# V copies moved to GpSimd, an earlier first cast of the keys, global-query work two slots later, and a last tile in other banks

## The chip, the cores and the metric

One core of a Trainium2 chip runs the whole kernel. The metric is the device time of one execution in microseconds (us); less is better. Engines are named as in the profile: PE is TensorE's matmuls and PEld its weight loads, DVE is VectorE, ACT is ScalarE, POOL is GpSimd, SP is SyncE, which here only issues DMAs. POOL issues DMAs as well.

## The reference

Two layers, cut to what is computed:

```python
# attention: B=8, H=8, 512 local tokens, 32 global tokens, head size 64
k_all = concat([k_g, k_l]); v_all = concat([v_g, v_l])
out_g = softmax(scale * q_g @ k_all.T) @ v_all                # global queries see all keys
s_ll  = where(|i - j| <= 32, scale * q_l @ k_l.T, -1e9)       # local queries: a band of 32 each way
out_l = softmax(concat([scale * q_l @ k_g.T, s_ll])) @ v_all  # and the 32 global keys
x = concat([out_g, out_l]) as (4352, 512)
# mixture of 8 experts, weights P by 8 rounds of Sinkhorn on exp(x @ w_gate)
out = sum over e of P[:, e] * (relu(x @ w1[e]) @ w2[e])       # 512 -> 1024 -> 512
```

## The kernel before

Attention works in units: unit n is one pair of heads (hp = n % 4) of one batch (b = n // 4), 32 in all. A loop over slots s = 0..33 writes out the order of the work by hand, and each engine runs its own instructions strictly in that order. In slot s stand the scores of unit s, the following steps of units s-1 and s-2, and the preparation of unit s+1:

- st_A(n): PE transposes keys and queries of unit n; DVE writes the keys to a buffer kTe (L279), ACT writes the queries to qbd (L283). There are four kTe buffers, used in turn.
- st_B(n, part): scores in three parts (PE L299, L301), masked on DVE (L306, tile ms), exponentials on ACT (L309, tile Pu).
- st_D1(n): a copy of the global part (DVE L315, tile Pl), transposes of the local part (PE L318), copied by DVE (L320, tile pw).
- st_D2(n, n2): transposes of Pl for n (ACT copy pg, L334) and of the finished rows xn for n2 into xT (ACT L336).
- st_E(n): the products with V (PE L352), written here E(n). They read V in two alignments, va and vb, and the global V in vgz; DVE divides (L356, L357). The result sits in the pool ps_po, which has one buffer.
- Global queries come in 16 groups j of four heads: st_G1 (scores on PE L371 in the same pool ps_po, maximum on DVE L373, exponential on ACT L376), st_G2 (transposes L384, ACT copy pgs L386, one buffer), st_G3 (products L396, L397; DVE L399 and L406 and ACT L409 write xgn). G1 of group j stands in slot 2j+2, G2 and G3 in slot 2j+3. st_G4 transposes xgn.
- keep_busy(n): n filler matmuls (L465).
- f1 and f2, from slot 5: first and second layer of experts 0 and 1 (L435, L449) for batches whose attention is done. Their rows go to memory by SP (yd).

V of a batch is loaded into va by POOL's DMAs (load_v: first, mid), a small piece into vb (last); the rest of vb is a copy of va to other partitions (part). For batch 0 one half of this copy runs on POOL in slot 1 (L177, L178) and the other on DVE in slot 2 (L180), just ahead of E(0); for batch 1 both halves run on POOL in slot 4. From batch 2 on, SP's DMAs make the copy and load vgz (move), in the slot before the batch's first.

Before slot 0 stand the first loads, memsets on DVE (clear), band masks on POOL (L258), the casts of the first queries and keys to fp16 (L470), st_A(0), the transposes of the global keys (cast L211, then L218, L220) and st_A(1). After the attention come the Sinkhorn rounds and experts 2 to 7 in a form with fewer products (L768, L864). The very last second-layer tile is computed by plain (L835) in two halves of 256 columns that lie in two banks of one tile, each read by DVE (L838).

Of the kernel before, what the change touches and what calls it, by code (L numbers as in the profile page):

```python
# [10 lines left out]
FP16 = mybir.dt.float16  # L11
FP32 = mybir.dt.float32
# [11 lines left out]
def kernel(  # L24
# [13 lines left out]
    nc = tc.nc  # L38

    B, H, Sl, Dh = q_l.shape  # L40
# [87 lines left out]
    with ExitStack() as att:  # L128
# [8 lines left out]
        kgT = att_c.tile([P, HP, B * Sg], FP16)  # L137
        qgT = att_c.tile([P, HP, B * Sg], FP16)
        qbd = [att_c.tile([P, NHB, P], FP16, name=f"qbd{i}") for i in range(2)]
        kTe = [att_c.tile([P, W + Sl + W], FP16, name=f"kTe{i}") for i in range(4)]  # L140
        vgr = [att_c.tile([P, 4 * H * VW], FP16, name=f"vgz{i}") for i in range(2)]
        vgz = [t.rearrange("p (a h v) -> p a h v", a=4, h=H) for t in vgr]
        vab = [(att_c.tile([P, NJ, H, VW], FP16, name=f"va{i}"),
# [16 lines left out]
        def load_v(b):  # L160
            va, vb = vab[b % 2]
            vz = vgz[b % 2]
            src = v_l[b].rearrange("h s d -> s h d")

            def first():
                nc.gpsimd.dma_start(out=vg16[b], in_=v_g[b].rearrange("h g d -> g h d"))
                nc.gpsimd.dma_start(out=va[W:P, 0, :, 0:Dh], in_=src[0:96])

            def mid(j):
                nc.gpsimd.dma_start(out=va[:, j, :, 0:Dh], in_=src[P * j - W : P * j + 96])  # L170

            def last():
                nc.gpsimd.dma_start(out=vb[HB : HB + W, NJ - 1, :, 0:Dh], in_=src[Sl - W : Sl])

            def part(eng, lo):
                if lo:
                    eng.tensor_copy(out=vb[96:P, NJ - 1], in_=va[W : 2 * W, 0])  # L177
                    eng.tensor_copy(out=vb[0:HB, :], in_=va[HB:P, :])  # L178
                else:
                    eng.tensor_copy(out=vb[HB:P, 0 : NJ - 1], in_=va[0:HB, 1:NJ])  # L180

            def move():
                if b < 2:
                    return part
                nc.sync.dma_start(out=vb[96:P, NJ - 1], in_=va[W : 2 * W, 0])
                nc.sync.dma_start(out=vb[0:HB, :], in_=va[HB:P, :])
                nc.sync.dma_start(out=vb[HB:P, 0 : NJ - 1], in_=va[0:HB, 1:NJ])
                if b > 1:
                    load_vz(b)

            return [first] + [lambda j=j: mid(j) for j in range(1, NJ)] + [last, move]
# [30 lines left out]
        def run(steps):  # L222
            for f in steps:
                f()
# [7 lines left out]
                eng.dma_start(out=fh[t][:, h], in_=src[0, h].rearrange("(p s) d -> p s d", s=NJ))  # L232
        load_gf(0, "kgs", f0[:, 2, :], (nc.sync, nc.scalar, nc.sync, nc.scalar))
        load_gf(0, "qgs", f0[:, 3, :], (nc.sync,) * 4)
        run(load_qk(0, 2, 4, H))
        nc.vector.memset(ones_f, 1.0)
        nc.scalar.activation(out=ones_f[:, 0:1], in_=ones_f[:, 0:1], func=AF.Exp, scale=0.0)
        nc.vector.memset(mask, 0.0)
# [6 lines left out]
        def clear(i, eng):  # L245
            va, vb = vab[i]
            eng.memset(va[0:W, 0], 0.0)
            eng.memset(va[:, :, :, Dh:VW], 1.0)
            eng.memset(vb[:, :, :, Dh:VW], 1.0)
            eng.memset(vgr[i].bitcast(mybir.dt.uint32), 0)  # L250
            for j in range(4):
                eng.memset(vgz[i][W * j : W * (j + 1), j, :, Dh:VW], 1.0)

        clear(0, nc.vector)
        for a in range(2):
            band = mask[HB * a : HB * (a + 1), 1, 0:KW]
            for base, m, c in ((0, -1, 1), (2 * W, 1, -1)):
                nc.gpsimd.affine_select(out=band, in_=band, compare_op=ALU.is_ge, fill=NEG, base=base,  # L258
                                        pattern=[[c, KW]], channel_multiplier=m)
        *steps, move = load_v(0)  # L260
        part = move()
        steps[0]()
        load_vz(0)
        run(steps[1:])
        clear(1, nc.gpsimd)

        st = {}

        def st_A(n):
            b, hp = divmod(n, HP)  # L270
            qs, ks = staged[b]
            qb, kt = qbd[n % 2], kTe[n % 4]
            pt = [ps_tr.tile([P, Sl], FP16, tag="tr", name="pk"), ps_sc.tile([P, Sl], FP16, tag="sc", name="pq")]
            for t, src in enumerate((ks, qs)):
                for so in range(NJ):
                    for a in range(2):
                        nc.tensor.transpose(pt[t][HB * a : HB * (a + 1), P * so : P * (so + 1)],  # L277
                                            src[:, 2 * hp + a, so, :], identity)
            nc.vector.tensor_copy(out=kt[:, W : W + Sl].rearrange("c (p s) -> c p s", s=NJ),  # L279
                                  in_=pt[0].rearrange("c (s p) -> c p s", s=NJ))  # L280
            for a in range(2):
                r = slice(HB * a, HB * (a + 1))
                nc.scalar.copy(out=qb[r, :, HB * a : HB * (a + 1)].rearrange("c i (p s) -> c i p s", s=NJ),  # L283
                               in_=pt[1][r].rearrange("c (s i p) -> c i p s", s=NJ, i=NHB))

        def st_B(n, part):
            b, hp = divmod(n, HP)
            qb, kt = qbd[n % 2], kTe[n % 4]
            if part == 0:
                st[n] = dict(Pu=att_wk.tile([P, NHB, SW], FP16, tag="Pu", name="Pu"),  # L290
                             mx=att_wk.tile([P, NHB], FP32, tag="mx", name="mx"))
# [70 lines left out]
        def st_G1(b, g):  # L362
            n0 = HP * b + 2 * g
            gc = slice(Sg * b, Sg * (b + 1))
            sg = ps_po.tile([P, 2 * 512], FP32, tag="po")
            for c0, c1, k0 in ((0, Sl - W, 2 * W), (Sl - W, Sl, W), (Sl, S, None)):
                for hh in range(4):
                    pr, a = divmod(hh, 2)
                    r = slice(HB * a, HB * (a + 1))
                    rhs = kgT[r, 2 * g + pr, gc] if k0 is None else kTe[(n0 + pr) % 4][r, k0 : k0 + c1 - c0]  # L370
                    nc.tensor.matmul(sg[W * hh : W * (hh + 1), c0:c1], qgT[r, 2 * g + pr, gc], rhs, start=True, stop=True)  # L371
            m2 = att_wk.tile([P, 2], FP32, tag="m2")
            nc.vector.reduce_max(out=m2[:, 0:1], in_=sg[:, 0:S], axis=AX.X)  # L373
            nc.vector.tensor_scalar(out=m2[:, 1:2], in0=m2[:, 0:1], scalar1=-scale, scalar2=None, op0=ALU.mult)
            Pg = att_wk.tile([P, S], FP16, tag="Pg")
            nc.scalar.activation(out=Pg, in_=sg[:, 0:S], func=AF.Exp, scale=scale, bias=m2[:, 1:2])  # L376
            gs[(b, g)] = Pg
# [88 lines left out]

        queue = []
        NU = B * HP
        for t in range(2):
            (nc.vector.tensor_copy if t else nc.scalar.copy)(out=staged[0][t][:, 0:2], in_=fh[t])  # L470
        nc.vector.tensor_copy(out=mask[:, 0, 0:KW], in_=mask[:, 1, 0:KW])
        nc.vector.tensor_copy(out=mask[:, 2, 0:KW], in_=mask[:, 1, 0:KW])
        nc.vector.memset(mask[:, 0, 0:W], NEG)
        nc.vector.memset(mask[:, 2, 3 * W : KW], NEG)
        st_A(0)
        cast_g("kgs")
        transpose_g(0, "kgs")
        st_A(1)
        for s in range(NU + 2):
            b, hp = divmod(s, HP)  # L480
            if s < NU and b + 1 < B:
                if hp == 0:
                    queue = load_qk(b + 1, 0, 4, H)
                if hp == 2:
                    *loads, move = load_v(b + 1)
                    queue += loads
                if hp == 3:
                    if s == 3:
                        part = move()
                    else:  # L490
                        queue = [move] + queue
                if s == 4:
                    queue += [lambda: wts.__setitem__(1, [load_w1(1)]), lambda: part(nc.gpsimd, True),
                              lambda: part(nc.gpsimd, False), lambda: wts[0].append(load_w2(0))]
# [3 lines left out]
                    queue += [lambda: wts[1].append(load_w2(1))]  # L498
                take = 0 if s == 0 else 2 if s >= 8 and hp < 2 else len(queue)
                if s == 1:  # L500
                    queue += [lambda: part(nc.gpsimd, True), load_first]
                    take = len(queue)
                for i, f in enumerate(queue[:take]):
                    f()
# [29 lines left out]
                    p_l2(*l2[n2], eng)  # L534
                    n2 += 1

            g_odd = s % 2 == 1 and 3 <= s <= NU + 1
            if g_odd:
                gb, gg = divmod((s - 3) // 2, 2)
            even = s % 2 == 0 and 2 <= s <= NU  # L540
            f1("a")
            if s < NU:
                st_B(s, 0)
            if even:
                st_G1(*divmod((s - 2) // 2, 2))
            if 1 <= s <= NU:
                st_D1(s - 1)
            if g_odd:
                st_G2(gb, gg)
            f2("a")  # L550
            if s < 7:
                st_B(s, 1)
# [6 lines left out]
            f1("a")  # L559
            if 0 < s < 7:  # L560
                st_A(s + 1)
            if s == 2:
                part(nc.vector, False)
                st_E(0)
            if s == 3:
                st_D2(None, 1)
            if s == 0:
                cast_g("qgs")
            if s == 1:
                transpose_g(0, "qgs")  # L570
            f1("v")
            if s < NU:
# [1 line left out]
            if s + 1 < NU and s >= 7:  # L574
                st_A(s + 1)
            if s == 2:
                keep_busy(3)
            if 2 <= s <= NU:
                st_E(s - 1)
            f2("a")  # L580
            if s >= 6 and (s - 6) % 4 == 0:
                logits(NJ * ((s - 6) // 4), NJ)
            if g_odd:
                st_G3(gb, gg)
            if s == 8:
                transpose_g(1, "kgs")
                transpose_g(1, "qgs")
            if s == 18:
                st_G4(0)
            f1("v")  # L590
            if 1 <= s < 5:
# [66 lines left out]
    with tc.tile_pool(name="tpool", bufs=2) as tpool, \  # L658
# [169 lines left out]
        def plain(u, last):  # L828
            order = sorted(range(FT), key=lambda fk: (fk % HF == HF - 1, fk))
            for j in range(2):  # L830
                zz = ps_z.tile([P, 2, D], FP32, tag="z", name="zp")
                for i, (d0, d1) in enumerate(((0, H2), (H2, D)) if last and j else ((0, D),)):
                    z = zz[:, i, :]
                    for n, fk in enumerate(order):
                        nc.tensor.matmul(z[:, d0:d1], u.a[2 * j + fk // HF][:, fk % HF, :], work["last"][:, fk, d0:d1],  # L835
                                         start=(n == 0), stop=(n == FT - 1), skip_group_check=True)
# [208 lines left out]
```

## Time and profile before

| | |
|---|---|
| Median of 3 runs | 1020.97 us (1020.89 to 1021.79) |
| The profiled execution's own time | 1019.79 us |
| Its span in the profile | 1018.0 us |
| Granted TensorE clock, mean of the span | 0.998 |
| PE idle in slot 2 (18.75 to 27.96) | 2.06 us |
| Start of slot 8 | 65.59 us |
| Last group's G1, G3 | 315.21 us, 329.68 us |
| Last DVE read of the last tile | 1014.28 us, 0.48 us long |

A row of the timeline is: start in us from the start of the span, duration in us, engine, line of the kernel, operation, the tile written and those read, shape, and the number of merged instructions; in brackets the idle time of that engine before it and who ended it.

### The profile page before, as it was taken

The page shows a single profiled execution, that of the slowest core. Times are in us where ns is not written, and L with a number is a line of the kernel's source. Part 1 is how long each engine was busy: PE and PEld are TensorE (multiplying, and loading weights), DVE is VectorE, ACT ScalarE, POOL GpSimd, SP SyncE. Part 2 cuts the span into 40 slices and gives each one's busy share as a digit, 9 for nine tenths or more (in the row PEclk, how much of TensorE's full clock was granted, in tenths as well). Part 3 has the DMA queues.
Part 4 walks back from the last instruction along what each step waited for, and adds up shares of the span by engine and source line. Part 5 has one row for each costly group of instructions (what it writes and reads, how often), then busy time and mean ns, then how long its engine had stood idle before and what let it go on. Part 6 is the DMA issues. An engine that isn't in the chain of part 4 may idle for free.

```text
span 1018.0 us, 22071 instructions
## 1 busy us (share of the span) xinstructions
PE 992.3 (97%) x8673; PEld 644.0 (63%) x8673; DVE 780.4 (77%) x1892; ACT 636.0 (62%) x1348; POOL 296.1 (29%) x357
## 2 busy tenths in 40 slices
PE   5899999999999999999999999999999999999997
PEld 3556666665655545666666666676767676766764
DVE  7776666666664563789999888997889999888885
ACT  6777777777775556765555555556765555555551
POOL 9547886778870022111111111111111111100000
PEclk9999999999999999999999999999999999999999
DMA  9999999999961297564443333466665533123043
GB/s 170 176 169 176 203 214 224 200 193 213 228 167 42 125 236 189 141 154 120 114 114 73 73 73 73 115 184 159 156 145 119 117 75 87 48 68 73 1 105 125
DMA packets 135881, 138.40 MB, mean 136 GB/s; under 512 B 54432, under 2 KB 107872, under 8 KB 133728
## 3 DMA queue, kind: packets, MB, share of 16 engines
q0 software_dynamic: 105696, 87.32, 49.0%
q1 hardware_dynamic: 29248, 49.28, 15.1%
q8 instruction: 68, 1.11, 0.4%
q10 hardware_dynamic: 832, 0.39, 0.1%
q14 instruction: 37, 0.30, 0.1%
HBM read 144.20 MB, written 39.58 MB: 181 GB/s over the span
## 4 chain that ended last, share of the span: by engine, by line
PE 92%; DVE 3%; DMA 2%; POOL 1%; ACT 1%; issue 1%; DVEq 0%; POOLq 0%; ACTq 0%
PE z L768 29%; PE pa L864 17%; PE py L449 11%; PE ph L435 11%; PE pb L864 9%; PE pc L864 5%; DMA va<-in_v_l_dram 2%; PE zp L835 1%; PE po L352 1%; PE sc L299 1%; PE ptw L318 1%; PE pk L277 1%; PE tgx L328 1%; PE po L396 1%; DVE ms L306 1%
## 5 line engine op out<-in xcount | busy, mean ns | idle before, releaser
L768 PEld LDWEIGHTS <-hs 128*128 128x128 f16 x2264 | 220.7, 98 | 92.8 <-issue 1.1
L768 PE MATMUL z<-w2e,hs 128*128 128x256 f16 x1304 | 195.6, 273 | 0.9 <-DVE oy L802 0.9
L768 PE MATMUL z<-v,hs 128*128 128x256 f16 x960 | 144.0, 273 | 0.0
L435 PE MATMUL ph<-xT,w1e 128*128 128x512 f16 (+1 forms) x576 | 129.6, 367 | 2.1 <-DVE lg L424 1.4
L449 PE MATMUL py<-w2e,hT 128*128 128x512 f16 x544 | 128.2, 379 | 0.4 <-DVE hT L440 0.4
L789 ACT COPY z<-z 128x256 f32<-128x256 f32 x98 | 35.0, 357 | 141.9 <-PE z L768 141.9
L864 PEld LDWEIGHTS <-w1e 128*128 128x128 f16 x960 | 86.6, 97 | 57.8 <-issue 1.6
L864 PE MATMUL pa<-t,s 128*128 128x512 f16 x384 | 114.2, 379 | 0.2 <-ACT s L889 0.2
L684 POOL DMA_DIRECT2D w1e<-in_moe_w_dram x24 | 17.4, 733 | 306.2 <-PE pa L864 230.3
L309 ACT ACTIVATE Pu<-ms,mx 128x160 f16<-128x160 f32 x256 | 92.2, 424 | 21.7 <-DVE mx L306 19.0
L802 DVE SCALAR_TENSOR_TENSOR oy<-z,lg,oy 128x512 f32<-128x512 f32 x128 | 95.8, 748 | 7.4 <-ACT oy L807 5.2
L764 DVE TENSOR_TENSOR hs<-hs 128x512 f16<-128x512 f16 x224 | 94.9, 424 | 8.2
L306 DVE CUSTOM_DVE_ANT_0 ms<-sc,mask 128x160 f32<-128x160 f32 x256 | 70.0, 320 | 36.3 <-PE sc L301 36.0
L868 DVE CUSTOM_DVE_ANT_0 hx<-pb,s 128x512 f16<-128x512 f32 x96 | 65.9, 686 | 39.7 <-ACT s L898 31.5
L684 POOL DMA_DIRECT2D w2e<-in_moe_w_dram x24 | 19.8, 830 | 242.4 <-PE z L768 212.2
L880 ACT ACTIVATE hs<-pc 128x512 f16<-128x512 f32 x96 | 57.2, 596 | 52.8 <-PE pc L864 52.8
L435 PEld LDWEIGHTS <-w1e 128*128 128x128 f16 x576 | 53.9, 98 | 52.6 <-issue 2.9
L868 DVE CUSTOM_DVE_ANT_0 hs<-pb,s 128x512 f16<-128x512 f32 x96 | 65.8, 686 | 27.7 <-ACT s L898 27.3
L864 PEld LDWEIGHTS <-s 128*128 128x128 f16 x720 | 65.6, 98 | 29.8 <-issue 1.8
L449 PEld LDWEIGHTS <-hT 128*128 128x128 f16 x544 | 50.0, 98 | 51.9 <-issue 0.5
L440 DVE TENSOR_SCALAR hT<-ph 128x512 f16<-128x512 f32 x58 | 40.1, 691 | 47.8 <-PE ph L435 46.5
L120 POOL TENSOR_TENSOR psum<-pw 128x512 f16<-128x512 f16 x48 | 55.0, 1178 | 43.8 <-DMA pw<-in_moe_w_dram 43.8
(187 smaller groups left out, 1979.1 us busy)
## 6 DMA issues: line engine op xcount, KB each, us to landing
ys<-yd SPq DMA_DIRECT2D x68, 256.0 KB, 3.6
yd<-yst SPq DMA_DIRECT2D x16, 1024.0 KB, 5.4
pw<-in_moe_w_dram POOLq DMA_DIRECT2D x24, 512.0 KB, 10.0
kept<-psum POOLq DMA_DIRECT2D x24, 512.0 KB, 4.0
s<-kept POOLq DMA_DIRECT2D x12, 768.0 KB, 8.9
v<-kept POOLq DMA_DIRECT2D x12, 768.0 KB, 9.4
w1e<-in_moe_w_dram POOLq DMA_DIRECT2D x12, 512.0 KB, 5.5
w2e<-in_moe_w_dram POOLq DMA_DIRECT2D x12, 512.0 KB, 6.5
```

The source lines that it names most:

```text
L120: nc.gpsimd.tensor_tensor(out=o, in0=x, in1=y, op=op)
L306: nc.vector.tensor_tensor_reduce(out=ms[:, ii, :], in0=sc[:, SW * ii : SW * (ii + 1)], in1=mask[:, mi, :], scale=-scale, scalar=BIG, op0=A ...
L309: nc.scalar.activation(out=d["Pu"][:, i, :], in_=ms[:, ii, :], func=AF.Exp, scale=-1.0, bias=d["mx"][:, i : i + 1])
L435: nc.tensor.matmul(ph[:, 0:n], wts[e][0][:, dk, P * fm : P * (fm + 1)], xT[:, dk, c0 : c0 + n], start=(dk == 0), stop=(dk == DP - 1))
L440: nc.vector.tensor_scalar(out=hT[:, fm, 0:n], in0=ph[:, 0:n], scalar1=0.0, scalar2=None, op0=ALU.max)
L449: nc.tensor.matmul(py, hT[:, fk, P * c : P * (c + 1)], wts[e][1][:, fk, :], start=(fk == 0), stop=(fk == FT - 1))
L764: nc.vector.tensor_tensor(out=o, in0=x, in1=y, op=op)
L768: nc.tensor.matmul(o, lhs[:, fk, :], rhs[:, fk, :], start=(first and fk == 0), stop=(fk == HF - 1), skip_group_check=True)
L802: nc.vector.scalar_tensor_tensor(out=o, in0=z, scalar=p, in1=o, op0=ALU.mult, op1=ALU.add)
L864: nc.tensor.matmul(o, lhs[:, dk, P * f : P * (f + 1)], rhs[:, dk], start=(first and n == 0 and dk == 0), stop=(dk == HD - 1), skip_group_c ...
L868: nc.vector._custom_dve(TENSOR_ADD_SAT, out=self.to(i, j), in0=self.of(ps), in1=self.of(s), s0=BIG, s1=0.0)
L880: nc.scalar.activation(out=self.to(0, 0), in_=self.of(self.pc), func=AF.Relu)
```

## The change

- The second half of the V copy of batch 0 also runs on POOL, in slot 1, ahead of the load of the first expert's weights; DVE's copy in slot 2 is gone. Each half is cut into smaller copies (five in all instead of three), for batches 0 and 1.
- DVE's memsets of vgz come after the first casts instead of before (clear_z), and the casts stand ahead of POOL's masks in the text. POOL issues only two of its four first loads ahead of the masks. st_A(0) stands ahead of the mask copies on DVE.
- All work on global queries moves by two slots: G1 of group j in slot 2j+4, G2 and G3 in 2j+5. The last group stays within slots 32 and 33, so those hold groups 14 and 15. The keys are kept in six buffers kTe. The transposes of the global queries move from slot 1 to slot 2, G4 of the first half from slot 18 to 20.
- With them, for batches 2 to 7, the last load of V and the moves (last, move) go from the slots before the batch to the start of its first slot.
- E(0) goes behind the last score part of slot 2, without the three filler matmuls; E(1) goes from slot 2 to slot 3; the transposes of unit 1's rows from slot 3 to slot 4.
- The last tile is computed in three pieces (256, 128 and 128 columns), each with its own tile; the second and third are in the pool ps_mm.

```diff
-        kTe = [... for i in range(4)]
+        kTe = [... for i in range(6)]
                 if lo:
                     eng.tensor_copy(out=vb[96:P, NJ - 1], in_=va[W : 2 * W, 0])
-                    eng.tensor_copy(out=vb[0:HB, :], in_=va[HB:P, :])
+                    eng.tensor_copy(out=vb[0:HB, 0:2], in_=va[HB:P, 0:2])
+                    eng.tensor_copy(out=vb[0:HB, 2:NJ], in_=va[HB:P, 2:NJ])
                 else:
-                    eng.tensor_copy(out=vb[HB:P, 0 : NJ - 1], in_=va[0:HB, 1:NJ])
+                    eng.tensor_copy(out=vb[HB:P, 0:2], in_=va[0:HB, 1:3])
+                    eng.tensor_copy(out=vb[HB:P, 2], in_=va[0:HB, 3])
...
-        run(load_qk(0, 2, 4, H))
+        steps = load_qk(0, 2, 4, H)
+        run(steps[0:2])
...
+        def clear_z(i, eng):
             eng.memset(vgr[i].bitcast(mybir.dt.uint32), 0)
             for j in range(4):
                 eng.memset(vgz[i][W * j : W * (j + 1), j, :, Dh:VW], 1.0)
 
         clear(0, nc.vector)
+        for t in range(2):
+            (nc.vector.tensor_copy if t else nc.scalar.copy)(out=staged[0][t][:, 0:2], in_=fh[t])
+        clear_z(0, nc.vector)
...
+        run(steps[2:4])
...
-        for t in range(2):
-            (nc.vector.tensor_copy if t else nc.scalar.copy)(out=staged[0][t][:, 0:2], in_=fh[t])
+        st_A(0)
         nc.vector.tensor_copy(out=mask[:, 0, 0:KW], in_=mask[:, 1, 0:KW])
...
-        st_A(0)
         cast_g("kgs")
         transpose_g(0, "kgs")
         st_A(1)
         for s in range(NU + 2):
             b, hp = divmod(s, HP)
+            if hp == 0 and 8 <= s < NU:
+                last()
+                move()
             if s < NU and b + 1 < B:
...
                     *loads, move = load_v(b + 1)
+                    if s > 2:
+                        last = loads.pop()
                     queue += loads
-                if hp == 3:
-                    if s == 3:
-                        part = move()
-                    else:
-                        queue = [move] + queue
+                if s == 3:
+                    part = move()
...
                 if s == 1:
-                    queue += [lambda: part(nc.gpsimd, True), load_first]
+                    queue += [lambda: part(nc.gpsimd, True), lambda: part(nc.gpsimd, False), load_first]
...
-            g_odd = s % 2 == 1 and 3 <= s <= NU + 1
-            if g_odd:
-                gb, gg = divmod((s - 3) // 2, 2)
-            even = s % 2 == 0 and 2 <= s <= NU
+            later = [divmod(j, 2) for j in ([s // 2 - 2] if 4 <= s <= NU + 1 else []) + ([NU // 2 - 1] if s >= NU else [])]
+            even, odd = ([], later) if s % 2 else (later, [])
             f1("a")
             if s < NU:
                 st_B(s, 0)
-            if even:
-                st_G1(*divmod((s - 2) // 2, 2))
+            for g in even:
+                st_G1(*g)
             if 1 <= s <= NU:
                 st_D1(s - 1)
-            if g_odd:
-                st_G2(gb, gg)
+            if s == 3:
+                st_E(1)
+            for g in odd[:1]:
+                st_G2(*g)
             f2("a")
...
-            if s == 2:
-                part(nc.vector, False)
-                st_E(0)
-            if s == 3:
+            if s == 4:
                 st_D2(None, 1)
             if s == 0:
                 cast_g("qgs")
-            if s == 1:
+            if s == 2:
                 transpose_g(0, "qgs")
...
             if s == 2:
-                keep_busy(3)
-            if 2 <= s <= NU:
+                st_E(0)
+            if 3 <= s <= NU:
                 st_E(s - 1)
             f2("a")
...
-            if g_odd:
-                st_G3(gb, gg)
+            for i, g in enumerate(odd):
+                if i:
+                    st_G2(*g)
+                st_G3(*g)
...
-                zz = ps_z.tile([P, 2, D], FP32, tag="z", name="zp")
-                for i, (d0, d1) in enumerate(((0, H2), (H2, D)) if last and j else ((0, D),)):
-                    z = zz[:, i, :]
+                for d0, d1 in ((0, H2), (H2, 3 * P), (3 * P, D)) if last and j else ((0, D),):
+                    z = ps_mm.tile([P, D], FP32, tag="mm", name="zq") if d0 else ps_z.tile([P, D], FP32, tag="z", name="zp")
```

More of the change, by code (lines that the diff above doesn't have):

```diff
@@ L139 @@
         qbd = [att_c.tile([P, NHB, P], FP16, name=f"qbd{i}") for i in range(2)]
-        kTe = [att_c.tile([P, W + Sl + W], FP16, name=f"kTe{i}") for i in range(4)]
+        kTe = [att_c.tile([P, W + Sl + W], FP16, name=f"kTe{i}") for i in range(6)]
         vgr = [att_c.tile([P, 4 * H * VW], FP16, name=f"vgz{i}") for i in range(2)]
@@ L265 @@
         clear(1, nc.gpsimd)
+        clear_z(1, nc.gpsimd)
         st = {}
@@ L271, in st_A @@
             qs, ks = staged[b]
-            qb, kt = qbd[n % 2], kTe[n % 4]
+            qb, kt = qbd[n % 2], kTe[n % 6]
             pt = [ps_tr.tile([P, Sl], FP16, tag="tr", name="pk"), ps_sc.tile([P, Sl], FP16, tag="sc", name="pq")]
@@ L287, in st_B @@
             b, hp = divmod(n, HP)
-            qb, kt = qbd[n % 2], kTe[n % 4]
+            qb, kt = qbd[n % 2], kTe[n % 6]
             if part == 0:
@@ L369, in st_G1 @@
                     r = slice(HB * a, HB * (a + 1))
-                    rhs = kgT[r, 2 * g + pr, gc] if k0 is None else kTe[(n0 + pr) % 4][r, k0 : k0 + c1 - c0]
+                    rhs = kgT[r, 2 * g + pr, gc] if k0 is None else kTe[(n0 + pr) % 6][r, k0 : k0 + c1 - c0]
                     nc.tensor.matmul(sg[W * hh : W * (hh + 1), c0:c1], qgT[r, 2 * g + pr, gc], rhs, start=True, stop=True)
@@ L587 @@
                 transpose_g(1, "qgs")
-            if s == 18:
+            if s == 20:
                 st_G4(0)
```

## The prediction

> **What bounds the kernel now.** I read the page's busy table first, then the windows by slot (a slot runs from its first score matmul, L299, to the next slot's), then the timeline at the places the diff touches.
>
> ```profile
> PE 992.3 (97%) x8673; PEld 644.0 (63%) x8673; DVE 780.4 (77%) x1892; ACT 636.0 (62%) x1348; POOL 296.1 (29%) x357
> ```
> ```profile
> 18.75:27.96 9.21, 7.15 (x128) 4.36 (x128) 7.00 (x30) 5.61 (x14) 6.20 (x9) 0.83 1.35 184
> 27.96:34.30 6.34, 5.41 (x98) 4.28 (x97) 4.75 (x24) 5.27 (x13) 4.64 (x7) 0.98 2.07 153
> 34.30:41.33 7.03, 5.19 (x96) 3.40 (x95) 6.37 (x25) 5.75 (x16) 6.97 (x9) 1.00 1.38 209
> ...
> 107.46:117.42 9.96, 9.96 (x123) 5.88 (x122) 6.44 (x26) 7.55 (x17) 6.36 (x8) 1.00 1.17 274
> ```
> The columns are the stretch, its length, busy PE, PEld, DVE, ACT, POOL, then the granted clock. Slots 2, 3 and 4 leave PE idle for 1 to 2 us each: there the chain PE, DVE, ACT, PE sets the pace. Slot 12, like nearly all after 65 us, has PE busy throughout. So a shorter opening (slots 1 to 7) brings the end forward, and PE work or a PE stall after slot 8 moves the end by its full length. The opening's worst place is slot 2:
>
> ```profile
> 20.15 0.81 PE L465 MATMUL pm<-kgT,identity 128*128 128x512 f16 x3
> 23.04 0.85 DVE L180 COPY vb<-va 64x1560 f16<-64x1560 f16 x1
> 23.94 0.22 PE L352 MATMUL po<-vb,pw 128*64 128x65 f16 x1 [1.57 <-DVE vb L180]
> 24.74 1.44 PE L465 MATMUL pm<-kgT,identity 128*128 128x512 f16 x3
> ```
> PE waits 1.57 us for the V copy that DVE makes; the same three filler matmuls then take 1.44 instead of 0.81 us: PE has dropped to half clock (0.83 mean in that slot).
>
> **The change, part by part** (us, against the profiled execution's 1019.79; the median shown is 1.18 above it).
>
> *Start.* DVE clears vgz (0.93 + 0.51) after the first cast instead of before, so the cast at 5.43 comes about 1.4 earlier. But look at what is next:
>
> ```profile
> 5.43 0.43 DVE L470 CAST ks<-f 128x512 f16<-128x512 f32 x1
> 7.66 0.82 DVE L211 CAST kgs<-f 128x512 f16<-128x512 f32 x1 [0.37 <-DMA f<-in_k_g_dram]
> 8.54 0.61 PE L218 MATMUL pt<-identity,kgs 128*128 128x128 f16 x4 [1.56 <-DVE kgs L211]
> ```
> The first score matmul (10.07) stands behind these transposes, and they behind a DMA. Two loads of POOL move behind its mask selects (1.46), which thins the DMA queue a little: at best the 0.37 of idle and 0.40 of the cast's excess (the same cast takes 0.42 at 12.74) go. 0 to -0.8; I take -0.4.
>
> *Slot 2.* Out go the DVE copy (0.85), one E with its rr and xn (0.21 + 0.69), G1 with reduce and scale (0.72 + 0.15) and exp (0.71 on ACT), three fillers, the wait and the cold clock. In comes qgT (0.42 on DVE). What remains on DVE: 8 masked scores at 0.245 start to start, 1.96; Pl 0.22; pw 0.68; kTe 0.69; qgT 0.42; rr and xn 0.90; together 4.9. ACT has 8 exps at 0.355, pg 0.35 and qbd 1.18, 4.4. To DVE I add 0.5 for a conflict with the V copies now on POOL, which this pair shows:
>
> ```profile
> 35.97 1.48 POOL L180 COPY vb<-va 64x1560 f16<-64x1560 f16 x1
> 36.44 1.10 DVE L315 COPY Pl<-Pu 128x256 f16<-128x256 f16 x1
> ```
> A DVE copy of 0.22 (as at 42.62) lasted until POOL's copy ended, 0.88 too long. The bounds are 0 and one whole short copy, about 1.0; only Pl of unit 1 falls under the copies. Slots 3 and 4 last 1.20 and 1.10 times their busiest engine; so 5.4 becomes 5.4 to 6.5, and I take 5.9: 9.21 - 5.9 = -3.3 (-2.7 to -3.8).
>
> *POOL's copies themselves.* From 16.36 they take 0.61 + 1.91 + 1.48 and two more starts, to about 20.6; before, PE reached E(0) at 22.17, and it now stands behind one more score block. (Slot 1 loses the qgT transposes, worth 0: slot 2 starts when ACT ends qbd, 18.69.) Cost 0; were that cover gone, each us late is a us of slot 2. Behind them on POOL the w1 load and the V loads of batch 1 start about 1.7 later; w1 landed 15 us before its first use at 44.65, and the copies for E(4) had ended at 37.45 against 46.24, so 0.
>
> *Slots 3 to 7.* Slot 3 gains E(1) (0.90 on DVE) and loses G2, G3 (ACT 0.69 + 0.62, DVE 0.73) and one xT; slot 4 gains that xT (0.59 on ACT, its second engine); slots 5 to 7 keep one part of a group each. +0.2 (-1.0 to +1.0).
>
> *End of attention.* Each pair of G slots moves two later, so one group's PE work leaves the opening for the PE-bound part, and slots 32 and 33 hold two groups. The last group of before:
>
> ```profile
> 315.71 0.72 DVE L373 TENSOR_REDUCE m<-sg 128x1 f32<-128x544 f32 x1 [0.57 <-PE sg L371]
> ...
> 316.71 0.71 ACT L376 ACTIVATE Pg<-sg,m 128x544 f16<-128x544 f32 x1 [0.81 <-DVE m L374]
> ...
> 324.69 0.69 ACT L386 COPY pgs<-pt 128x640 f16<-128x640 f16 x1
> ...
> 331.31 0.62 ACT L409 ACTIVATE xgn<-po,rg 32x64 f16<-32x64 f32 x2 [0.84 <-PE ph L435]
> ```
> Work: G1 holds PE from 315.21 to 315.56, G2 from 324.00 for 0.28, G3 from 329.68 for 0.56: +1.2. First wait: both G1 of slot 32 use the one buffer of ps_po; the second may start when the first's exp is done, 317.42, while PE is free at 315.56: +1.9, with D1 and all matmuls of the slot queued behind. Second wait: in slot 33 G3(14), G2(15), G3(15) follow each other. PE is through G2(15) at 330.24 + 0.28 = 330.52, but ACT copies its result after xgn of group 14 (ends 331.93), plus 0.69: 332.62. +2.1. Together +5.2; 4.3 if ACT gets the copy in ahead of half of that, 5.6 with another wake-up each.
>
> *Last tile.*
> ```profile
> 1011.80 1.36 DVE L838 SCALAR_TENSOR_TENSOR o<-zp,lg,o 128x512 f32<-128x512 f32 x2 [0.97 <-PE zp L835]
> 1013.21 1.03 PE L835 MATMUL zp<-w2e,hs 128*128 128x256 f16 x8 [0.58 <-DVE o L838]
> 1014.28 0.48 DVE L838 SCALAR_TENSOR_TENSOR o<-zp,lg,o 128x256 f32<-128x256 f32 x1 [1.13 <-PE zp L835]
> ```
> Separate tiles remove the 0.58 wait. From 1012.65 two pieces of 8 x 128 columns at about 0.06 (the eight 128-wide transposes at 28.28 take 0.46) end at 1013.65; DVE on 128 columns, from 0.75 and 0.48 for 512 and 256, is 0.35: 1014.04 against 1014.76. -0.7 (-0.2 if each matmul waits for a weight load, 98 ns in the page).
>
> *Loads in another place.* The V moves of batch b go from slot 4b-1 to the start of 4b, on SP behind a yd store, and one load on POOL waits there for G3. From first big vb issue to last vgz landing took 13.4 (87.94 to 101.31); E(12) at 123.14 leaves 17.2 after the G3 that frees the buffer (105.9). Cost 0.
>
> Sum: -0.4 - 3.3 + 0.2 + 5.2 - 0.7 = **+1.0**: 1020.8 for a run like the profiled one, 1022.0 as a median.
>
> **Rivals.** *The clock falls after a new stall (slower).* In slot 2 the fall at 24.77 followed a stretch of 3.4 us with 1.5 us of PE work in it; the half clock lasted 3.4. The new stalls of 1.9 and 2.1 leave 1.5 or less in a stretch that holds one whole. Where PE is never idle, 3.4 at half clock costs 1.7: 1023.7 for one stall, 1025.4 for both. It decides by whether a stretch catches the whole stall, about 1.4 in 3.4 for each, and by whether dense matmuls around it count for more than slot 2's transposes. [...]
>
> *The opening gives more (faster).* All terms at their good ends: -0.8 - 3.8 - 1.0 + 4.3 - 0.8 = -2.1, 1018.9. For it: PE idles 1.8 in slot 4 as well. Against: ACT and DVE stay at 5 us and more there.
>
> *The vb moves land late (slower).* The yd store ahead of them took 9.0 (105.99 to 114.97). If they wait for all of it, 3.8 of slack becomes 5 of stall in some of five slots: +10, 1032. Against: the DMA engines are nearly idle just before (121 to 122, 101 to 103), and POOL's loads wait in that spot too.
>
> **The numbers.** Forecast 0.55, clock 0.28, faster opening 0.12, late moves 0.05. About 0.2% (2.0 us) is what a measurement can tell from no change. The forecast's own spread of 1.3 around +1.0 puts 0.40 within it, 0.13 above, 0.02 below; the clock rival 0.22 above, 0.06 within; the opening rival 0.07 below, 0.05 within; late moves 0.05 above. Faster 0.09, same 0.51, slower 0.40. The range, 1019.0 to 1025.4, runs from the good end of the opening to both clock falls.
>
> **What would show it.** Right: no wait for vb in slot 2, clock 1.00 there, slot 8 starting some 3.5 earlier; one PE wait near 312 for Pg and one near 327 for pgs, about 2 each; L838 three times at the end with no PE wait. Wrong: slot 2 longer than 6.5; no such waits at the end; a granted clock under 1.00 after 300; PE waiting for vb or vgz in slots 9, 13, 17.

## The result: 0.33% slower, and the profile after

| | before | after |
|---|---|---|
| median (21 runs each) | 1020.55 us | 1023.53 us |
| ratio, 95% interval | | 1.0033 (1.0022 to 1.0045) |
| profiled execution, span | 1019.79, 1018.01 | 1022.25, 1020.47 |
| start of slot 8 | 65.59 | 60.25 |
| slots 8 to 30 | 239.63 | 241.51 |
| from slot 31 to the end | 712.79 | 718.71 |

Of the 21 runs of after, 12 show a mean granted clock of 0.998 (median 1024.65) and 9 one of 1.000 (1022.34). A stretch of 3.41 us at half clock, as in the last row below, costs 1.7 us of work, and 1.7 of 1020 is what 0.998 stands for.

The busy table of after: PE has the same work as before and waits elsewhere.

```profile
PE 992.0 (97%) x8678; PEld 644.0 (63%) x8678; DVE 781.3 (77%) x1896; ACT 636.8 (62%) x1348; POOL 297.9 (29%) x362
```

The windows by slot of after (slots 2, 4 and 26, then a stretch in slot 32; columns as before):

```profile
18.63:23.66 5.03, 4.18 (x84) 3.17 (x84) 3.97 (x22) 4.37 (x12) 4.97 (x8) 1.00 1.08 139
...
29.94:36.08 6.14, 5.06 (x100) 3.60 (x100) 4.88 (x24) 5.29 (x14) 5.13 (x8) 1.00 2.04 171
...
248.64:260.34 11.70, 10.68 (x140) 6.36 (x139) 8.26 (x27) 7.65 (x17) 9.59 (x11) 1.00 1.52 228
314.19:317.60 3.41, 3.41 (x26) 1.94 (x19) 1.61 (x4) 0.71 (x1) 0.00 (x0) 0.50 0.00 0
```
Slot 2 went from 9.21 to 5.03 at full clock, slot 4 from 7.03 to 6.14; slot 3 takes 6.28 (6.34). Slot 12 is at 9.96 as it was, but slot 26, which took 10.78 before, takes 11.70 with PE idle for 1.0: a loss in a stretch that the prediction left at zero. In the last row PE is busy throughout at half clock.

The timeline of after in slot 2: POOL's last V copy, and E(0), which no longer waits for vb.

```profile
20.00 0.61 POOL L182 COPY vb<-va 64x520 f16<-64x520 f16 x1
...
22.59 0.22 PE L362 MATMUL po<-vb,pw 128*64 128x65 f16 x1
```

At the start, DVE in after: the cast of the global keys stands where it stood (7.66 before), now behind its own engine's mask steps (from 7.12 on; the last is shown) instead of a DMA.

```profile
7.54 0.09 DVE L483 MEMSET mask<- 128x32 f32 x1
7.68 0.68 DVE L213 CAST kgs<-f 128x512 f16<-128x512 f32 x1
```

The end of attention, in the timeline of after:

```profile
313.26 0.71 ACT L386 ACTIVATE Pg<-sg,m 128x544 f16<-128x544 f32 x1 [0.80 <-DVE m L384]
314.02 0.50 PE L381 MATMUL sg<-kTe,qgT 64*32 64x480 f16 x8 [1.85 <-ACT Pg L386]
...
331.73 0.62 ACT L419 ACTIVATE xgn<-po,rg 32x64 f16<-32x64 f32 x2 [0.84 <-DVE xgn L416]
332.38 0.69 ACT L396 COPY pgs<-pt 128x640 f16<-128x640 f16 x1
333.13 0.62 PE L406 MATMUL po<-vb,pgs 128*128 128x260 f16 x4 [2.02 <-ACT pgs L396]
```
Both waits are where the prediction put them: G1(15) for the one ps_po buffer, G3(15) for a copy that stands behind xgn on ACT. The half clock begins 0.17 after the first wait ends.

The last tile in after, PE's two pieces of 128 columns and DVE's three reads; PE waits for none:

```profile
1015.81 1.06 PE L843 MATMUL zq<-w2e,hs 128*128 128x128 f16 x16
1016.01 0.48 DVE L846 SCALAR_TENSOR_TENSOR o<-zp,lg,o 128x256 f32<-128x256 f32 x1
1016.46 0.80 DVE L846 SCALAR_TENSOR_TENSOR o<-zq,lg,o 128x128 f32<-128x128 f32 x2
```

Last, the place the prediction had nothing for: slot 26, a plain copy on DVE beside POOL's sums for the later experts (form of sums, L120) and POOL's load ahead of them.

```profile
250.47 0.83 POOL L106 DMA_DIRECT2D pw<-in_moe_w_dram  x1
250.74 1.83 DVE L325 COPY Pl<-Pu 128x256 f16<-128x256 f16 x1
251.24 2.35 POOL L120 TENSOR_TENSOR psum<-pw 128x512 f16<-128x512 f16 x2
252.63 0.28 PE L342 MATMUL tgx<-identity,Pl 128*128 128x128 f16 x2 [0.73 <-DVE Pl L325]
```
The copy takes 0.22 when alone (42.62 in before). Here it begins during POOL's DMA issue and ends at 252.57, 0.09 after the first of the two sums (251.24 to 252.48). The other four over 1 us after slot 8 do the same (1.01 at 134.48, 1.31 at 166.19, 1.69 at 208.22, 1.11 at 218.94): each ends 0.08 to 0.10 after a sum.

### The profile page after: what moved, and what is told of

Same layout as the page of the kernel before. It is cut to its first block, busy times and chain, and to the rows that moved or that the text cites. A ratio compares the mean times of both kernels' runs of the same rounds, so it can differ in the third digit from the quotient of the medians.

```text
span 1020.5 us, 22080 instructions
## 1 busy us (share of the span) xinstructions
PE 992.0 (97%) x8678; PEld 644.0 (63%) x8678; DVE 781.3 (77%) x1896; ACT 636.8 (62%) x1348; POOL 297.9 (29%) x362
## 3 DMA queue, kind: packets, MB, share of 16 engines
q8 instruction: 68, 1.11, 0.4%
## 4 chain that ended last, share of the span: by engine, by line
PE 92%; DVE 4%; ACT 2%; issue 1%; DMA 0%; ACTq 0%; DVEq 0%
PE z L777 29%; PE pa L872 17%; PE ph L445 11%; PE py L459 11%; PE pb L872 9%; PE pc L872 5%; PE sc L309 1%; PE po L362 1%; PE zp L843 1%; PE ptw L328 1%; DVE ms L316 1%; PE pk L287 1%; DVE Pl L325 1%; PE po L406 1%; PE pq L287 1%
## 5 line engine op out<-in xcount | busy, mean ns | idle before, releaser
L906 ACT COPY s<-pa 128x512 f32<-128x512 f32 x102 | 59.8, 586 | 12.2 <-PE pa L872 1.1
```

The source lines that it names most:

```text
L906: nc.scalar.copy(out=self.pre3, in_=self.pa)
```

## Experiments

In the tables "8 to 30" is the time from the start of slot 8 to the start of slot 31 and "end" from there to the end of the span, both of one profiled execution; "ratio" is to the kernel before, with its 95% interval. The diffs are cut to the lines that matter.

### The two waits at the end

Edits, against after:

```diff
 g1_apart                                   # G1(15) behind the slot's last f2
-            for g in even:
+            for g in even[:1]:
                 st_G1(*g)
...
             f2("a")
+            for g in even[1:]:
+                st_G1(*g)
 g2_early                                   # G2(15) behind the first f2, pgs in two buffers
+            for g in odd[1:]:
+                st_G2(*g)
...
-            for i, g in enumerate(odd):
-                if i:
-                    st_G2(*g)
+            for g in odd:
                 st_G3(*g)
 both_apart                                 # both edits
 fillers                                    # matmuls in front of the waiting ones
+                if i: keep_busy(8)         # before G1(15)
+                    keep_busy(9)           # before G3(15)
```

> The changed kernel, with G1 of group 15 behind the last second-layer piece of slot 32 instead of right behind G1 of group 14. If the 1.85 us wait for Pg is a cost of its own, it goes and nothing takes its place: PE idle near 312 to 314 falls from 1.85 to under 0.2, and slot 33 comes 1.8 earlier against the changed kernel, 3.5 where that kernel also lost 1.7 to the half clock behind this wait. Times: 1.9 to 3.5 below the changed kernel, so 1020 to 1021.6. If PE only finds the same wait elsewhere (E of unit 31, or G2 of group 14), the idle time moves and the time stays.

> The changed kernel, with G2 of group 15 behind the first second-layer piece of slot 33 and two pgs buffers, so that G3 of group 15 finds its operand ready. If the 2.02 us wait for pgs is a cost of its own, PE idle near 333 goes and the time is 2.0 lower (1021.5). The wait for Pg near 314 and the half clock behind it stay. If the wait is set by something else than ACT's order (the one pgs buffer, the bank), some of it stays.

> Both edits. By the theory of the stalls the sum is 1.85 + 2.02, and the half clock of 3.4 us after slot 32, worth 1.7, has no more cause: 3.9 to 5.6 below the changed kernel, 1018 to 1019.6, that is 1 to 2.5 below the kernel before; granted clock 1.00 over the span in all its runs. If the loss of the changed kernel lies elsewhere, it stays above the kernel before.

> The changed kernel, with 8 filler matmuls (1.7 us) in the wait ahead of G1 of group 15 and 9 (1.9 us) in the wait ahead of G3 of group 15. The waits themselves stay. If the half clock comes from the idle stretch, no half clock is recorded after slot 32, the granted clock of all runs is 1.00 over the span, and the time is about 1.7 below those runs of the changed kernel that had it, about 1.0 in the median (1022.5). If the half clock comes from something else (the phase of a window, the load), it appears as often as before, and the fillers change nothing or add up to 0.3.

| | median | ratio | 8 to 30 | end |
|---|---|---|---|---|
| after | 1023.53 | 1.0033 | 241.51 | 718.71 |
| g1_apart | 1021.37 | 1.0005 (0.9992, 1.0017) | 243.83 | 715.32 |
| g2_early | 1021.85 | 1.0019 (1.0005, 1.0033) | 244.28 | 715.20 |
| both_apart | 1018.61 | 0.9985 (0.9975, 0.9994) | 243.34 | 713.37 |
| fillers | 1022.96 | 1.0025 (1.0015, 1.0034) | 244.88 | 717.08 |

The forecasts for g1_apart and both_apart held (1020 to 1021.6, 1018 to 1019.6); g2_early and fillers came 0.35 and 0.46 above theirs (1021.5, 1022.5).

PE's waits from 300 to 340 in both_apart (total us, times, longest one):

```profile
PE py L459 <- DVE hT L450: 0.6, 1, 0.6
PE ph L445 <- DVE lg L434: 0.3, 1, 0.3
```
Each edit removes its wait and leaves the other at 1.85 or 2.02; both remove both. The end falls by 5.34 = 1.85 + 2.02 + 1.47, the last part being the half clock. With the fillers G1(15) comes just as late:

```profile
315.44 1.90 PE L475 MATMUL pm<-kgT,identity 128*128 128x512 f16 x8
317.36 0.40 PE L381 MATMUL sg<-kTe,qgT 64*32 64x480 f16 x8
```
From G1(14), at 315.09, to G1(15) it is 2.27 here and 2.27 in after; but the clock stays at 1.00 and the end is 1.63 shorter. All 11 runs of fillers show 1.000, against 9 of 21 in after. So the waits cost time as waits, and the half clock that the first brings is a separate price of some 1.6.

In the profiles of g1_apart and g2_early the half clock is absent, each with one wait left. But 2 of the 12 runs of g1_apart and 7 of the 12 of g2_early have a mean clock of 0.998 or less, and none of the 22 runs of both_apart and fillers, so it does not seem to need both waits. Two later kernels of this document, which keep both, show it in their traces: pool_free has it behind the first wait alone (from 319.05), no_sums behind the second alone (from 341.25). What differs fits the prediction's idea of a stretch that catches the whole wait. Where a trace has two half-clock stretches, their starts lie 37.54 (before_no_sums), 51.19 (no_sums) and 116.05 (pool_free) apart, which is 11, 15 and 34 times 3.413 (3.4127, 3.4127 and 3.4132); the one in after lasted 3.41. With the span cut at that pitch, the stretches just ahead of a half clock held 0.35 to 1.68 us of PE work (1.53 in before, 1.56 in after). Those that caught one of the two waits less fully, with 1.78 (no_sums, first wait), 1.82 (g2_early) and 1.92 (pool_free, second wait), had full clock behind them. One does not fit: 331.26 to 334.67 in after, at the second wait, held 1.54 and the clock stayed at 1.00. So the moment at which the wait falls seems to decide; the exact rule stays open.

The four kernels and after keep the same order of work up to slot 31, and yet their slots 8 to 30 take 241.5 to 244.9. Something there costs 2 to 5 us against the 239.63 of before, and differs from profile to profile.

### Which part gave the opening

Edits: v_copy_only is the kernel before with nothing but the V copies in five pieces on POOL; g_old_slots is after with the global work at the slots of before; before_again is the kernel before, once more.

```diff
 v_copy_only, against before                # and the pieces of part, as in the change
-                    queue += [lambda: part(nc.gpsimd, True), load_first]
+                    queue += [lambda: part(nc.gpsimd, True), lambda: part(nc.gpsimd, False), load_first]
...
-                part(nc.vector, False)
                 st_E(0)
 g_old_slots, against after
-            later = [divmod(j, 2) for j in ... ]
+            later = [divmod(s // 2 - 1, 2)] if 2 <= s <= NU + 1 else []
...
-            if s == 2:
+            if s == 1:
                 transpose_g(0, "qgs")
```

> The kernel before, with nothing but the second half of the V copy of batch 0 made by POOL in slot 1, in the five short copies. If the DVE copy's place was what made PE wait in slot 2 and drop to half clock, the 1.57 us wait goes, slot 2 has a clock of 1.00 and takes 6.5 to 7.5 instead of 9.2, and the time is 1.5 to 2.5 below the kernel before. If the wait only passes to POOL's copies, which end near 20.6, or to pg on ACT, slot 2 stays over 8.

> The changed kernel with G1, G2, G3 and the transposes of the global queries back in the slots of the kernel before; all else stays, the late moves of V among it. By the theory of the end stalls, the part after slot 31 is as before less the 0.9 of the last tile (711.9), with no half clock. In the opening the group returns: slot 8 at 61.5 to 63 instead of 60.3. Slots 8 to 30 tell who causes the collisions: if POOL's new order (the load that waits for G3 at the first slot of a batch) does, they still take 241.5 to 245; if the place of the global work does, 239.6. Sum 1016 to 1019.5.

> The kernel before, profiled once more, for how its stages vary. If the half clock in slot 2 follows from the 1.57 us wait there and from where a stretch of 3.4 us begins, slot 2 takes 8 to 9.2 with or without it, and slots 8 to 30 between 239.3 and 240.3.

| | median | ratio | slot 8 at | 8 to 30 | end |
|---|---|---|---|---|---|
| v_copy_only | 1017.07 | 0.9976 (0.9965, 0.9988) | 61.27 | 240.18 | 712.67 |
| g_old_slots | 1016.37 | 0.9964 (0.9951, 0.9978) | 61.11 | 240.19 | 711.79 |
| before_again (one run) | 1019.19 | | 63.42 | 241.08 | 712.87 |

Slot 2 of v_copy_only, in the windows:

```profile
18.52:24.75 6.23, 5.63 (x128) 3.81 (x128) 5.70 (x29) 5.46 (x14) 6.17 (x9) 1.00 1.17 153
```
The V copies alone bring slot 8 from 65.59 to 61.27, four fifths of what the whole change brings. The kernel before varies here itself: its profile had the half clock in slot 2; in before_again slot 2 took 7.90 without it, so some 1.3 of the 4.3 was the clock, and from its 63.42 the V copies bring 2.15 of 3.17, two thirds. The wait did go, as expected, and the gain was larger than expected: slot 2 took 6.23 (6.5 to 7.5), and the median is 3.1 below the 1020.20 of before in the same comparison (1.5 to 2.5). before_again missed both of its ranges (7.90 for 8 to 9.2, 241.08 for 239.3 to 240.3): two profiles of one program differ by 1.45 in slots 8 to 30.

The later global work buys 61.11 - 60.25 = 0.86 more in the opening; behind it, after takes 1.32 more than g_old_slots in slots 8 to 30 and 6.92 more in the end. g_old_slots is the fastest of all kernels tried: it keeps the V copies, the earlier cast, the late moves, the six buffers and the last tile (end 711.79 against 712.79), and leaves the global work alone. It is 0.7 below v_copy_only, with overlapping intervals, and the profiles of both are of their fastest runs (1014.95 and 1015.89). Its 240.19 lies nearer to the 239.6 expected if the place of the global work brings the loss than to the 241.5 of POOL's new order. The late moves have no slack left in it: in batches 3 to 5 the last landing of vgz comes 0.07 to 0.20 after E's first use begins, by the trace's landing times; a later landing would make E wait, which its profile does not show.

### What slots 8 to 30 lost

First try: let ACT make the copy Pl from unit 7 on, alone and on top of both_apart.

```diff
-            nc.vector.tensor_copy(out=d["Pl"], in_=d["Pu"][:, :, KW:SW])
+            (nc.vector.tensor_copy if n < 7 else nc.scalar.copy)(out=d["Pl"], in_=d["Pu"][:, :, KW:SW])
```

> The changed kernel, with the copy of Pl (L325) made by ACT instead of DVE from unit 7 on. Theory: in slots 8 to 30 the changed kernel loses 1.9 to 5 us because this copy, from SBUF to SBUF, waits until a sum on POOL is through, and PE waits for it. Then slots 8 to 30, 241.5 to 244.9 long in the five profiles with the late moves, take 239.0 to 240.0 here, PE waits for Pl are gone, and the time is 2 to 4 below the changed kernel (1019.5 to 1021.5). Rival: ACT, busy 8 of 10 us in these slots, cannot take 25 more copies of about 0.35; then PE waits for ACT instead and the length stays over 241.

> The version with both groups' steps apart at the end (label both_apart), and the copy of Pl on ACT from unit 7 on. If the losses add, this is its 1018.6 less 2 to 4: 1014.6 to 1016.6, 0.4 to 0.6% below the kernel before. If ACT becomes late, it equals both_apart.

| | median | ratio | 8 to 30 | end |
|---|---|---|---|---|
| pl_act | 1021.51 | 1.0019 (1.0011, 1.0028) | 242.00 | 717.31 |
| both_pl_act | 1017.65 | 0.9978 (0.9969, 0.9986) | 242.00 | 713.60 |

No copy is long any more and the two profiles give the same 242.00, but the even slots now pay 0.26 each, in which PE waits for ACT's Pl: 10.22 and 11.04 instead of 9.96 and 10.78. In slot 12 of pl_act ACT makes Pl behind an exponential of 0.71 and ends it at 106.44, and PE's transposes of it start at 106.50. So the rival came true, and both_pl_act missed its 1014.6 to 1016.6. The edit takes the chance out and puts a fixed price in.

Second try: why do the collisions come in after? The waits of POOL from 66 to 300, before and then after:

```profile
POOL vb L173 <- PE po L397: 5.7, 4, 2.2
```
```profile
POOL vb L173 <- PE po L407: 14.7, 5, 3.9
```
The load last writes vb, which G3 of the batch before last still reads. With G3 two slots later and the load behind it, POOL's queue stands there five times (14.7 us), at the end of slots 11, 15, 19, 23 and 27. My reading was that everything queued behind it is shifted by that, to the same place of the same slots: in slots 14, 18, 22 and 26 a load issue and then the first sum 2.1 to 2.7 after the slot's start, where Pl stands. This covers three of the five slots that lost time in after (18, 22 and 26, 2.06 of 2.64); in slots 15 and 23 the sum had waited for its weights to land. In g_old_slots the late load is there as well, but not the late G3, and POOL's waits have no such row. So pool_free takes the wait away: the 32 rows go to a tile of their own, two slots earlier, and SP moves them into vb.

```diff
+        vl = att_c.tile([P, H, Dh], FP16, name="vl")
...
-                last()
                 move()
...
-                nc.gpsimd.dma_start(out=vb[HB : HB + W, NJ - 1, :, 0:Dh], in_=src[Sl - W : Sl])
+                o = vb[HB : HB + W, NJ - 1, :, 0:Dh] if b < 2 else vl[HB : HB + W]
+                nc.gpsimd.dma_start(out=o, in_=src[Sl - W : Sl])
...
+                nc.sync.dma_start(out=vb[HB : HB + W, NJ - 1, :, 0:Dh], in_=vl[HB : HB + W])
```

> The changed kernel, with the last 32 rows of V of batches 2 to 7 loaded by POOL two slots earlier into a tile of their own, and put into vb by SP with the other moves, so that POOL never waits for G3. Theory: this wait (1.7 to 3.9 us in the changed kernel's profile) is what brings POOL's sums under DVE's copy of Pl in slots 10, 14, 18, 22, 26. Then slots 8 to 30 take 239.6 to 240.5, as in the version with the global work at its old slots, where POOL does not wait either; the end keeps both waits (718.7 with the half clock, 717 without); time 1.5 to 4 below the changed kernel. Rival: the place of the global work itself makes PE need Pl earlier in these slots; then they still take over 241.5.

It was slower: 1026.8, ratio 1.0062 (1.0047 to 1.0077), 245.72 in slots 8 to 30. Slots 18, 22 and 26 are back at 10.78, as the theory had it (slot 14, which was at 10.78, takes 10.97), but others collide instead. The worst, slot 21:

```profile
199.01 0.76 POOL L106 DMA_DIRECT2D pw<-in_moe_w_dram  x1
199.78 2.27 POOL L120 TENSOR_TENSOR psum<-pw 128x512 f16<-128x512 f16 x2
```
```profile
199.00 3.15 DVE L328 COPY Pl<-Pu 128x256 f16<-128x256 f16 x1
```
```profile
202.80 0.44 PE L341 MATMUL tgx<-identity,xn 128*128 128x128 f16 x4 [2.21 <-DVE pw L333]
```
One copy of 0.22 was held through the load issues and two sums in a row, PE waited 2.21, and half clock followed (203.0 to 206.4): slot 21 took 14.35 for 10.34. So the wait for G3 bears on where the collisions lie in after, but a kernel without it has them elsewhere; that half of the theory fell. It is not a clean trial either. vl has one buffer, and POOL's one wait for it, 1.01, stands just ahead of this collision. POOL now also waits at other loads, 2.6 and 4.5 for va and 5.0 for qs, which it does not in after. And of the other slow slots (13 and 19, 11.41 and 11.07 for 10.34) slot 13 has 0.55 of PE waiting for vgz to land.

Third try: take the sums away, in both kernels. The four operations at L120 are left out and their tile is cleared once.

> The kernel after, without POOL's four subtractions and additions per block of expert weights (their rows are cleared once and stored as zeros; all loads and stores stay), so experts 2 to 7 compute something else in the same time. Theory (DVE's copies Pl wait for POOL's sums, and that is all that slots 8 to 30 lost): no copy Pl over 0.5 us after slot 8 except one under the clearing, and slots 8 to 30 take 239.0 to 239.7 us against 241.51 to 244.9 with the sums; the two waits after slot 31 (1.85 and 2.02) stay. Rival (the new order on PE or the late loads cost those slots something by themselves): over 241.

> The kernel before, with the same sums left out in the same way. Theory: slots 8 to 30 take 239.0 to 239.7 us here too, the same as in the kernel after without sums within 0.3, against 239.63 and 241.08 in the two profiles with sums. Rival (the order of the global work matters by itself): over 1 us less than the kernel after without sums.

| | median | ratio | 8 to 30 | end |
|---|---|---|---|---|
| no_sums (after) | 1028.01 (3 runs) | 1.0093 (1.0058, 1.0127) | 249.34 | 718.23 |
| before_no_sums | 1020.92 | 1.0000 (0.9980, 1.0019) | 238.65 | 712.77 |

For before the theory holds and its figure was a little high: 238.65, with no slot off its pace. So the sums cost the kernel before 1.0 (239.63) to 2.4 (before_again). (Its median does not show that, since clearing the tile held a copy for 2.85 at 58.25 and PE for 3.07 in slot 7, and a half clock followed.) For after the number was a miss, and a telling one. All its slots but three keep their pace; slot 8 holds the clearing (+1.32), and slots 13 and 29 wait for a landing (+0.88 and +8.27, in slot 29 with half clock from 290.06 to 296.89). Without those three amounts it is 238.87, 0.2 from before. So the new order on PE costs these slots 0.2 (slot 20, 10.19 for 9.96), and what is lost there with sums is 2.6 to 6.0 (241.51 to 244.88 in five profiles).

The five profiles themselves show that this lies in the held copies. Every slot that lost 0.1 or more holds a copy Pl of 0.87 or longer, but for slot 17 of g1_apart and g2_early (0.13 each), and an even slot loses what its copy took beyond some 0.92: 1.83 and 0.91 (after, slot 26), 2.50 and 1.58 (g1_apart, slot 18), 2.64 and 1.72 (g2_early, slot 30). Not all of it is the sums. In slot 10 of four of the five (all but after) the copy ends 0.12 to 0.17 after a row of load issues, with no sum through yet:

```profile
82.06 2.65 POOL L170 DMA_DIRECT2D va<-in_v_l_dram  x3
83.29 2.30 DVE L325 COPY Pl<-Pu 128x256 f16<-128x256 f16 x1
```
That is g1_apart; the last issue, of 0.79, begins at 84.68, and the slot lost 1.38. In the four, slot 10 lost 0.39 to 1.38. In after the copy of slot 10 began at 83.10, 0.07 into an issue of the same row, and took 0.22: a shift of a few tenths decides. no_sums has these issues too, but at other places, so it does not clear them.

Slot 29 of no_sums is the rival that the prediction gave 0.05:

```profile
288.57 0.19 PE L361 MATMUL po<-vgz,pg 128*64 128x65 f16 x1 [1.86 <-DMA vgz<-vg]
...
293.18 0.21 PE L361 MATMUL po<-vgz,pg 128*64 128x65 f16 x1 [2.59 <-DMA vgz<-vg]
```
```profile
270.69 0.93 POOL L120 DMA_DIRECT2D kept<-psum  x1
...
272.21 0.92 POOL L120 DMA_DIRECT2D kept<-psum  x1
```
```profile
273.07 5.00 SPq L157 DMA_DIRECT2D vgz<-vg  x4
```
With no sums between them POOL's stores and loads of 512 KB come in a row, just ahead of the moves of vgz, and the two queues take 74.6% and 22.9% of the DMA engines' time from 270 to 300; the last landing was at 293.1. In after the same landings are early enough, but barely. By the trace's landing times, E's first use of vgz came after the last landing by

| batch | 3 | 4 | 5 | 6 | 7 |
|---|---|---|---|---|---|
| before | 21.9 | 22.3 | 24.8 | 22.0 | 21.5 |
| after | 0.7 | 1.4 | 1.2 | 0.3 | 5.7 |

## The prediction, point by point

- **Start, -0.4: gained 0.12.** The DMA wait of the kgs cast went, but DVE's four mask steps were moved into its place and end at 7.63. The prediction counted the edge that went and not what is next on the same engine, which was in its own list of moves; the cast takes 0.68 instead of 0.82, so only 0.14 of its excess of 0.40 went.
- **Slot 2, -3.3: gained 4.18.** Right in kind: no wait, full clock, E(0) at 22.59. The size was off, outside -2.7 to -3.8. DVE was busy for 3.97 in the slot and not 4.9: the prediction counted all of xn, of which 0.64 runs behind the slot's end (from 23.61). The 0.5 for a conflict was not needed in this run, by luck: Pl (19.92, 0.22) came just as a V copy ended (20.05). In both_apart, whose slot began 0.54 earlier, Pl took 0.75 and the slot 5.55.
- **Slots 3 to 7, +0.2: gained 1.05**, nearly all of it in slot 4, whose Pl took 1.10 under a V copy of 1.48 and takes 0.38 now, the shorter copies of batch 1 falling into slot 5 (Pl 0.45 there). The prediction showed that row, but used it only as a price for slot 2 and not as a gain where it stood.
- **End of attention, +5.2: waits 1.85 and 2.02** against 1.9 and 2.1. Right, and shown by taking each away. The work forecast at 1.2 is 1.2 to 1.5: what is left of the end's 5.92 + 0.88 after the two waits and a half clock of 1.7 or 1.47.
- **Last tile, -0.7: gained 0.88.** The last expert's second layer (z) begins 3.34 later than in before (1002.42 for 999.08) and the span ends 2.46 later; no PE wait is left there.
- **The clock rival came true** in the profiled run, at one of the two waits: a granted clock under 1.00 after 300, which the prediction named as a sign against itself. 12 of the 21 runs show a clock that fits one such stretch; where it lay in the runs without a profile no trace shows. It had 0.28; its price of 1.7 is what fillers gave back (1.63).
- **Loads in another place, 0: here a step failed.** The moves themselves cost nothing in after, as said, with no wait for vb or vgz in slots 9, 13 and 17; the slack of 3.8 was really 0.3 to 1.4 in four batches and 5.7 in the last, and no_sums shows what lies behind it. But the load that waits on POOL for G3 was looked at for its own landing alone, and not for what is queued behind it. What follows on POOL is load issues and sums, and these hold up DVE's copies: +1.9 against before in the profiled run, more in others. That the copies are what is lost is shown; that the wait for G3 is what brings them under POOL's work is argued, and pool_free speaks against its being the only cause.

The sum by the profile: -5.34 + 1.88 + 5.92 = +2.46, against +1.0. The opening gave 1.84 more than the forecast's -3.5, and slots 8 to 30 took 1.88 of it back; what is left over is the half clock. As a median the kernel is 2.98 above before, inside the range (1023.53 for 1019.0 to 1025.4), and past the bound of 0.2%: of the cases it is the clock rival's figure of 1023.7, with the collisions, which no case had, paid for by the opening. That the figure agrees to 0.2 is partly luck: two errors of 1.8 cancel.

## What to carry to other kernels

Steps that share one buffer and are put one after the other at the end of a pipeline paid their whole latency here (1.85 and 2.02), and a stall there could cost a half-clock stretch on top (3.41 long in after, some 1.6 of time); put other work between them (both_apart won 4.9 us of median by that). When POOL's queue is moved, price what stands in it, and that includes DVE copies like Pl that run beside its work, its load issues too (0.22 alone, 1.83 beside an issue and a sum in after, 2.30 beside issues in g1_apart). Try the parts alone: here one part gave two thirds to four fifths of the gain in the opening, and the part meant to go with it cost more than all of it.

## What the runs showed of the hardware

- A DVE copy of 256 fp16 per partition within SBUF, 0.22 alone, lasted 1.83 (after) and 3.15 (pool_free), until some 0.1 after one of POOL's operations ended. Between two of POOL's operations it was let in only sometimes: in after it came through behind the first of two sums, in pool_free it outlasted a load issue and both sums (the copy ended at 202.15, the sums at 202.05).
- Loads that POOL issues hold such a copy too: in the kernel before, the copy at 58.69 took 0.57 and ended 0.05 after an issue of 0.82, and in g1_apart the one at 83.29 took 2.30 under a row of issues. Not every issue does: in after one that began 0.07 into an issue (83.10) took its 0.22.
- Half clock came after a wait of 1.85 in the middle of dense matmuls, for 3.41 at a granted clock of 0.50 (after, 314.19 to 317.60), and in some runs only: 9 of the 21 have a mean clock of 1.000. With fillers of 1.90 and 2.11 in the two waits all 11 runs stayed at 1.00.
